# Windowed attention and a wave-MLP in one kernel: a new hand-written order with some copies on other engines

## The chip, the cores and the metric

The kernel runs on one core of a Trainium2 chip. The metric is the device time of one execution in microseconds; the median of three runs of the kernel before is 164.15 us (164.02 to 164.84).

## The reference

Four batches of 768 tokens and 8 heads of 64 go through attention and then through a mixing layer of width 512.

```python
scores = scale * np.matmul(q, k.transpose(0, 1, 3, 2))
is_global = pos[None, :] < 8
is_local = (rel >= 0) & (rel < 96)
dist = np.where(is_global & ~is_local, 96.0, np.abs(rel))
a = softmax(where(is_global | is_local, scores - slope[h] * dist, -1e9))
x = (a @ v), heads side by side                  # 768 x 512
theta = x @ w_theta
y = w_tok_r @ (x * cos(theta)) + w_tok_i @ (x * sin(theta))
u = x + y
out = u + np.maximum(u @ w_ch, 0.0)
```

A query sees itself, the 95 tokens before it and the first 8 tokens, so of the 768 x 768 scores only the diagonal tiles of 128 x 128 and the tiles beside them are computed.

## The kernel before

**Tiles.** Tokens are cut into 6 tiles of 128, heads into 4 pairs. Tokens are the partitions of x, u and the outputs; for the matmuls x and u are needed transposed (xT, uT). Batches are called 0 to 3.

**The order.** All five engines follow one order that is written out as a string at line 574. Each word names an operation and its indices: `s.1.2.0` calls `s_(1, 2, 0)`. The words are issued from left to right, and each engine runs its own instructions in that sequence. A second string at line 640 gives, word by word, the PSUM bank (of eight) that the next operation with a result in PSUM takes. An operation whose bank is still being read waits for that reader.

**Words, by stage.** b is the batch, p the head pair, i is 0 for q and 1 for k, and the letter v or a at the end names VectorE or ScalarE as the engine of a copy.

- Loads, issued by POOL (GpSimd): `lq` q and k (lines 77 and 86), `lv` v (line 92), `lw`, `lt`, `lc` the weights. Batch 3 is loaded token by token, in 16 transfers (`lq.3.0.4` and `lq.3.4.4`). Only q and k of batch 0, pair 0 come through SP and ScalarE's queue (line 103). `mv` (line 212) writes the column of ones of v before v is loaded.
- Bias: batch 0 adds the distance bias on TensorE (`sb`, lines 336 and 343, from `diag` and `dist`); the others multiply the exponentials by a table (`bt` makes it on ScalarE, line 153; `x` multiplies on VectorE, lines 383 and 386).
- `cast` (line 276) turns q and k of pair 0 to bf16. `q` (lines 291 and 294) transposes q or k on TensorE; `pc` (line 306) packs for that. `qe` (line 299) copies the result from PSUM to qT or kT; its last number is 2 for the whole and 0 or 1 for a half of the tokens. `pd` (line 312) does both for batch 3 as a transposing transfer issued by SP.
- `kg` (lines 322 and 323) makes kG: a copy of kT's tiles in which the first 8 columns are the global tokens, in two instructions for the tiles t0 to t1. `vg` (lines 397 and 398) does the same for v.
- `s` (line 362) computes scores into two banks, in three pieces c per head pair; `e` (line 374) is the exponential on ScalarE; `v` (line 421) multiplies by v, and `n` (lines 432 and 434) divides by the sum on VectorE and writes x.
- `xt` (line 451) transposes a pair of x on TensorE and `xe` (line 456) copies it; `xd` (line 443) does both as one transposing transfer issued by SP. x of batch 2, pair 3 goes by `xt.2.3` and `xe.2.3`; its pairs 0 to 2 go by `xd`.
- `w` and `we` (lines 265 and 269) transpose and copy the token weights, in batch 0.
- `th` (line 477) is theta, `sn` (lines 487 and 489) cosine and sine on ScalarE, `z` (line 498) the products on VectorE, `m` (line 511) the mixing over tokens, in three groups g for each output tile tt, `u` (line 519) the sum on VectorE. `sin` (line 257) is a sine of one column, which brings the activation table ahead.
- u is transposed by `ut` and `ue` (lines 535 and 539, TensorE and a copy) or by `ud` (line 529, a transposing transfer issued by SP). All of batch 0 goes by `ut`; so does the last tile, 3.5.
- `c` (line 550) multiplies by w_ch, `r` (line 560) does the maximum and the sum on VectorE, `st` (line 566) stores. The last number 2 is a whole tile of 128 x 512; 0 and 1 are its halves, and half 1 is stored from ScalarE's queue, the others from SP's. Only tile 3.5 goes in halves. `r` takes turns among 8 output buffers.
- `gt.1.2` (line 230) is a copy of one element of z of batch 1 on POOL. POOL stands there until z.1.1.0 has run, and `lq.3.4.4` is behind it.
- `warm` (line 237) are matmuls of zeros.

Of the kernel before, what the change touches and what calls it, by code (L numbers as in the profile page):

```python
# [16 lines left out]
def kernel(  # L17
# [105 lines left out]
    dist = const.tile([T, 6, T], BF)  # L123
# [13 lines left out]
    half = T // 2  # L137
# [6 lines left out]
    diag = const.tile([T, H, T], BF)  # L144
# [37 lines left out]
    ps_of = {}  # L182
# [147 lines left out]
    def sb_(p, c):  # L330
        pb = ps_of["s", 0, p, c] = ps_big()
        n = blocks(c)
        s0 = 2 if c else 0
        if p < 2:
            for hh in range(2):
                nc.tensor.matmul(pb[:, hh, 0:n * T], lhsT=diag[:, 2 * p + hh],  # L336
                                 rhs=dist[:, s0:s0 + n].rearrange("p s n -> p (s n)"),
                                 start=True, stop=False)
            return
# [8 lines left out]
    def s_(b, p, c):  # L348
        qT, kT, kG = qkT[b, p]
        if b:  # L350
            ps_of["s", b, p, c] = ps_big()
        pb = ps_of["s", b, p, c]
        for j in range(2):
# [3 lines left out]
            for part in range(2 if jt + 1 < NT else 1):  # L357
                for hh in range(2):
# [4 lines left out]
                                     start=bool(b), stop=bool(b) or (jt == NT - 1 or (j == 1 and part == 1)))  # L363
# [205 lines left out]
    def do(op, *a):  # L569
# [17 lines left out]
        xe.0.3.0.2.v bt.5 xt.0.2.0.6 xt.0.3.4.6 bt.3 xe.0.2.0.6.v th.0.0.4 we.0.0.v lv.1.0.8 bt.2
        we.1.0.v th.0.0.5 mv.2 th.0.0.3 we.1.1.v th.0.1.2 we.0.1.v sn.0.0.0 xe.0.3.4.6.v lq.2.0.8
        w.2.0 sn.0.0.1 z.0.0.0 th.0.1.3 th.0.2.2 sn.0.1.0 z.0.0.1 sn.0.1.1 w.3.0 z.0.1.0 th.0.2.3
        w.2.1 sn.0.2.0 z.0.1.1 m.0.0.0 m.0.1.0 sn.0.2.1 z.0.2.0 lv.2.0.8 w.3.1 pc.1.1.0 sin.0  # L590
        m.0.1.1 we.2.0.a z.0.2.1 we.3.0.a pc.1.0.0 m.0.0.1 q.1.1.0 we.2.1.v m.0.1.2 bt.1 q.1.0.0
        pc.1.0.1 m.0.2.0 qe.1.0.0.a.2 pc.1.1.1 qe.1.1.0.v.2 q.1.0.1 q.1.1.1 qe.1.0.1.a.2 m.0.0.2
        pc.1.3.0 pc.1.2.0 kg.1.0.0.4.a pc.1.3.1 q.1.3.0 u.0.1 m.0.2.1 qe.1.1.1.a.2 pc.1.2.1 we.3.1.v
        w.4.0 lq.3.0.4 kg.1.1.0.4.a u.0.0 q.1.2.0 m.0.2.2 qe.1.3.0.v.2 qe.1.2.0.a.2 ut.0.1 we.4.0.v
        s.1.0.0 ue.0.1.a s.1.0.1 u.0.2 w.4.1 e.1.0.0 w.5.1 we.4.1.v ut.0.0 q.1.2.1 e.1.0.1 ue.0.0.v
        q.1.3.1 qe.1.2.1.v.2 c.0.1.2 qe.1.3.1.a.2 we.5.1.v s.1.1.0 s.1.0.2 r.0.1.2 s.1.1.2 e.1.1.0
        c.0.0.2 kg.1.2.0.4.a x.1.1.0 m.0.3.0 x.1.0.1 e.1.1.2 m.0.4.0 r.0.0.2 e.1.0.2 m.0.3.1 x.1.0.2
        x.1.0.0 s.1.1.1 s.1.2.0 e.1.1.1 vg.1.0.8 m.0.3.2 kg.1.3.0.4.a w.5.0 m.0.4.1 x.1.1.1 e.1.2.0
# [24 lines left out]
        z.2.2.1 s.3.0.2 m.2.0.1 st.0.3.2 r.1.5.2 e.3.0.2 m.2.1.2 e.3.0.1 x.3.0.2 vg.3.0.8 s.3.1.0
# [60 lines left out]
```

## Time and profile before

| what | value |
|---|---|
| median of three runs | 164.15 us (164.02 to 164.84) |
| the profiled execution's own time | 164.6 us |
| its span, first to last instruction | 162.4 us |
| granted TensorE clock over the span | 1.00 |
| first theta matmul | 25.4 us |
| last matmul's end, last VectorE result, last store landed | 158.6, 159.1, 161.2 us |
| u transposing transfers, issue to landing | 17, median 2.5 us |
| x transposing transfers, issue to landing | 8, median 3.0 us |

The span is what the engines' rows cover; the execution's own time has 2.2 us around it. "Busy" is the union of an engine's rows. A row of the timeline gives start, duration, engine, line, operation and tiles, and in brackets the idle time before it with what ended that. The times in this text count from the start of the span.

### The profile page before, as it was taken

What the parts mean: (1) busy time and instruction counts of PE and PEld (TensorE: products, weight loads), DVE (VectorE), ACT (ScalarE), POOL (GpSimd) and SP (SyncE); (2) the same over time, 40 slices, a digit from 0 to 9 for tenths busy, and PEclk for the clock granted to TensorE, in tenths of its full rate; (3) what the DMA queues carried; (4) which work ended last, traced back from release to release, by engine and by line L of the source; (5) the groups of instructions that cost most, each with busy time, mean ns of one, the idle gap of its engine ahead of it and who ended that gap; (6) DMA issues with size and microseconds to landing.
All of it is one profiled execution on the core that took longest, in us unless ns stands there. A gap on an engine that the chain in (4) does not pass through costs nothing.

```text
span 162.4 us, 3831 instructions
## 1 busy us (share of the span) xinstructions
PE 156.0 (96%) x1575; PEld 87.1 (54%) x1575; DVE 123.7 (76%) x254; ACT 110.9 (68%) x148; POOL 38.3 (24%) x46
## 2 busy tenths in 40 slices
PE   7979999999999999999999999999999999999990
PEld 2446686556845586454655554445464544444450
DVE  7688998686989998997989682896987714736371
ACT  3978999999987897989987776898560339100010
POOL 8985248104408202029900000000000000000000
PEclk9999999999999999999999999999999999999999
DMA  4999999999999999929999996660679086003885
GB/s 140 211 165 177 206 209 205 203 210 200 157 176 204 168 131 151 197 56 84 133 130 136 197 164 151 129 178 4 145 228 128 12 238 160 4 0 76 248 286 198
DMA packets 71904, 25.14 MB, mean 155 GB/s; under 512 B 59984, under 2 KB 68944, under 8 KB 71888
## 3 DMA queue, kind: packets, MB, share of 16 engines
q0 software_dynamic: 45696, 12.45, 89.4%
q1 hardware_dynamic: 25776, 11.93, 33.5%
q10 hardware_dynamic: 416, 0.52, 0.9%
q8 instruction: 12, 0.20, 0.5%
q14 instruction: 4, 0.03, 0.1%
HBM read 25.69 MB, written 6.29 MB: 197 GB/s over the span
## 4 chain that ended last, share of the span: by engine, by line
PE 89%; DVE 7%; issue 1%; ACT 0%; DVEq 0%
PE bank L511 39%; PE bank L477 13%; PE bank L550 12%; PE bank L421 6%; PE bank L362 6%; PE bank L294 3%; PE bank L237 3%; PE bank L265 3%; PE bank L451 2%; PE bank L336 1%; DVE kG L322 1%; DVE qT L299 1%; DVE x_sb L434 1%; PE bank L535 1%; DVE kT L299 1%
## 5 line engine op out<-in xcount | busy, mean ns | idle before, releaser
L511 PE MATMUL bank<-zri,w_tokT 128*128 128x512 bf16 x288 | 68.8, 379 | 0.0
L374 ACT ACTIVATE e<-bank 128x1024 bf16<-128x1024 f32 (+1 forms) x48 | 43.2, 955 | 8.1 <-PE bank L362 7.7
L511 PEld LDWEIGHTS <-w_tokT 128*128 128x128 bf16 x288 | 26.4, 98 | 28.2
L498 DVE TENSOR_TENSOR zri<-x_sb,cs 128x1024 bf16<-128x1024 bf16 (+1 forms) x30 | 16.6, 581 | 10.6 <-ACT cs L489 5.5
L550 PE MATMUL bank<-w_ch_bf,uT 128*128 128x512 bf16 (+1 forms) x100 | 24.0, 371 | 0.0
L519 DVE TENSOR_TENSOR u<-x_sb,bank 128x512 bf16<-128x512 bf16 x24 | 16.3, 682 | 9.1 <-PE bank L511 9.1
L477 PE MATMUL bank<-w_theta_bf,xT 128*128 128x512 bf16 x96 | 22.8, 379 | 0.0
L560 DVE SCALAR_TENSOR_TENSOR o<-bank,u 128x512 f32<-128x512 f32 (+1 forms) x25 | 16.5, 665 | 2.5 <-PE bank L550 2.5
L434 DVE TENSOR_TENSOR x_sb<-bank,rec 128x768 bf16<-128x768 f32 (+2 forms) x21 | 16.1, 767 | 0.7
L383 DVE TENSOR_TENSOR e<-e,etab 128x1024 bf16<-128x1024 bf16 (+1 forms) x24 | 14.8, 635 | 1.5 <-ACT e L374 1.5
L539 ACT COPY uT<-bank 128x512 bf16<-128x512 bf16 x4 | 2.4, 592 | 18.2 <-PE bank L535 18.2
L550 PEld LDWEIGHTS <-uT 128*128 128x128 bf16 x100 | 9.4, 98 | 10.1 <-DMA uT<-u 0.5
L477 PEld LDWEIGHTS <-xT 128*128 128x128 bf16 x96 | 9.1, 98 | 9.7 <-DVE xT L456 0.2
L421 PEld LDWEIGHTS <-e 128*128 128x128 bf16 x352 | 12.6, 97 | 2.8 <-issue 0.2
L362 PE MATMUL bank<-qT,kT 64*128 64x128 bf16 x224 | 13.4, 218 | 0.0
L421 PE MATMUL bank<-vn,e 128*128 128x65 bf16 x224 | 12.7, 193 | 0.2
L489 ACT ACTIVATE cs<-bank,halfpi 128x1024 bf16<-128x1024 f32 x8 | 8.9, 1114 | 5.6 <-PE bank L477 5.6
L362 PEld LDWEIGHTS <-kT 64*128 64x128 bf16 x224 | 8.7, 94 | 7.0 <-issue 6.1
L92 POOL DMA_DIRECT2D vn<-in_v_dram x5 | 9.9, 1976 | 8.0 <-DVE qkn L306 7.1
L362 PE MATMUL bank<-qT,kG 64*128 64x128 bf16 x128 | 10.4, 216 | 0.9 <-DVE kG L323 0.9
L421 PE MATMUL bank<-vG,e 128*128 128x65 bf16 x128 | 10.3, 193 | 0.0
L86 POOL DMA_DIRECT2D qk<-in_q_dram x8 | 6.9, 857 | 10.7 <-issue 5.4
(77 smaller groups left out, 206.4 us busy)
## 6 DMA issues: line engine op xcount, KB each, us to landing
out_dram<-o SPq DMA_DIRECT2D x23, 256.0 KB, 2.4
vn<-in_v_dram POOLq DMA_DIRECT2D x3, 768.0 KB, 23.4
qk<-in_q_dram POOLq DMA_DIRECT2D x2, 768.0 KB, 20.6
qk<-in_k_dram POOLq DMA_DIRECT2D x2, 768.0 KB, 22.0
w_nat<-in_moe_w_tok_r_dram POOLq DMA_DIRECT2D x3, 384.0 KB, 12.7
w_nat<-in_moe_w_tok_i_dram POOLq DMA_DIRECT2D x3, 384.0 KB, 13.8
vn<-in_v_dram POOLq DMA_DIRECT2D x2, 384.0 KB, 10.1
qk<-in_q_dram POOLq DMA_DIRECT2D x8, 96.0 KB, 7.4
```

Source lines behind the costliest of these rows:

```text
L92: nc.gpsimd.dma_start(out=vn[:, h0:h0 + n, :, 0:D].rearrange("p h t d -> p (h t) d"), in_=v[b, h0:h0 + n].rearrange("h (t p) d -> p (h t) ...
L362: nc.tensor.matmul(pb[:, hh, o:o + T], lhsT=lhsT, rhs=qT[R, (own, nxt)[part]], start=bool(b), stop=bool(b) or (jt == NT - 1 or (j == 1 and ...
L374: nc.scalar.activation(e_c, ps_of["s", b, p, c][:, :, 0:blocks(c) * T], AF.Exp, scale=scale)
L383: nc.vector.tensor_mul(e_c, e_c, tab[:, :, s0:s0 + n].rearrange("p a s n -> p a (s n)"))
L421: nc.tensor.matmul(po4[:, head - h0, it - i0], lhsT=l_, rhs=r_, start=(i_ == 0), stop=(i_ == len(mms) - 1))
L434: nc.vector.tensor_mul(xv, po4[:, :, :, 0:D], rec.to_broadcast([T, m_, nt, D]))
L477: nc.tensor.matmul(ps_of["th", b, c][j_], lhsT=xT_sb[b][:, dc, (2 * c + j_) * T:(2 * c + j_ + 1) * T], rhs=w_theta_bf[:, dc, :], start=(dc ...
L498: nc.vector.tensor_mul(zri[b][:, i_, tt, :].rearrange("p j (g d) -> p j g d", g=NP), x_sb[b][:, :, tt, :].rearrange("p g j d -> p j g d"), ...
L511: nc.tensor.matmul(ps_of["m", b, tt], lhsT=w_tokT[wi][:, st, tt * T:(tt + 1) * T], rhs=zri[b][:, wi, st, :], start=(mixed[b, tt] == 0), st ...
L519: nc.vector.tensor_add(u_sb[b, tt].rearrange("p (g d) -> p g d", g=NP), x_sb[b][:, :, tt, :], ps_of["m", b, tt].rearrange("p (g d) -> p g ...
L550: nc.tensor.matmul(ps, lhsT=uTs[b, tt][:, dc, :], rhs=w_ch_bf[:, dc, own], start=(dc == 0), stop=(dc == NC - 1))
L560: nc.vector.scalar_tensor_tensor(o_sbs[b, tt][:, own], in0=ps_of["c", b, tt, part], scalar=0.0, in1=u_sb[b, tt][:, own], op0=ALU.max, op1= ...
```

## The change

- Pair 0 of batch 0: the two halves of q are copied by VectorE (`qe.0.0.0.v`), those of k by ScalarE, and the first tile of kG is made by ScalarE (`kg.0.0.0.1.a`).
- The copy `gt.1.2` is gone; `lq.3.4.4` stands before `th.1.0.6`, and `mv.3` and `lv.3.0.8` come after `s.2.0.2`.
- u tile 0.1 goes by `ud.0.1`, x pair 2.3 by `xd.2.3`.
- The output tiles 3.1 and 3.2 are computed, finished and stored in halves, in the last stretch of the order.
- kG of batch 2, pair 0 is made in two parts. Some other copies change between VectorE and ScalarE.
- The order and the banks are written anew throughout. The sequence of operations of one engine differs in most places.
- `sb_` has a new branch that no word of the order uses, and `s_` asks whether its banks were taken already, which gives the same as before.

The diff, cut to the functions, the order up to the first theta matmul, and the places that the text speaks of:

```diff
@@ -327,10 +327,18 @@
         return min(4, 2 * NT - 1 - 4 * c)
 
     @op
-    def sb_(p, c):
+    def sb_(p, c, rows=False):
         pb = ps_of["s", 0, p, c] = ps_big()
         n = blocks(c)
         s0 = 2 if c else 0
+        if rows:
+
+            for hh, r in ((0, 0), (1, 1), (0, 1), (1, 0)):
+                K = slice(r * half, (r + 1) * half)
+                nc.tensor.matmul(pb[:, hh, 0:n * T], lhsT=diag[K, 2 * p + hh],
+                                 rhs=dist[K, s0:s0 + n].rearrange("p s n -> p (s n)"),
+                                 start=(r == hh), stop=False)
+            return
         if p < 2:
             for hh in range(2):
                 nc.tensor.matmul(pb[:, hh, 0:n * T], lhsT=diag[:, 2 * p + hh],
@@ -347,7 +355,8 @@
     @op
     def s_(b, p, c):
         qT, kT, kG = qkT[b, p]
-        if b:
+        fresh = ("s", b, p, c) not in ps_of
+        if fresh:
             ps_of["s", b, p, c] = ps_big()
         pb = ps_of["s", b, p, c]
         for j in range(2):
@@ -360,7 +369,7 @@
                     lhsT = kG[R, jt - 1, :] if part and jt else kT[R, own]
                     o = (2 * j + part) * T
                     nc.tensor.matmul(pb[:, hh, o:o + T], lhsT=lhsT, rhs=qT[R, (own, nxt)[part]],
-                                     start=bool(b), stop=bool(b) or (jt == NT - 1 or (j == 1 and part == 1)))
+                                     start=fresh, stop=fresh or (jt == NT - 1 or (j == 1 and part == 1)))
...
-        warm.3.1 diag.0 diag.1 dist warm.6.0 bt.6 swap bt.0 cast.1.0.v cast.1.1.a sb.0.0 bt.7 sb.0.1
-        cast.0.1.a cast.0.0.v q.0.0.1 q.0.1.0 qe.0.0.1.a.0 q.0.0.0 qe.0.1.0.a.2 kg.0.0.0.1.v
-        warm.1.3 qe.0.0.1.v.1 qe.0.0.0.a.0 kg.0.0.1.4.v q.0.1.1 qe.0.0.0.a.1 s.0.0.0 lw.0
-        qe.0.1.1.v.2 s.0.0.1 e.0.0.0 sb.1.2 sb.1.0 kg.0.1.0.4.v lt.0.2 e.0.0.1 diag.2 s.0.1.0
-        q.0.2.1 lt.2.4 e.0.1.0 q.0.2.0 qe.0.2.1.v.2 s.0.1.2 sb.0.2 e.0.1.2 sb.1.1 kg.0.2.0.4.v
-        s.0.1.1 qe.0.2.0.v.2 sb.2.1 e.0.1.1 lw.2 s.0.0.2 vg.0.0.4 sb.2.0 e.0.0.2 q.0.3.0 diag.3
-        s.0.2.0 mv.1 s.0.2.1 qe.0.3.0.v.2 e.0.2.0 q.0.3.1 lq.1.0.8 sb.2.2 qe.0.3.1.v.2 e.0.2.1
-        v.0.1.1.0.6 v.0.1.0.0.6 v.0.0.0.0.6 n.0.1.1.0.6 kg.0.3.0.4.a v.0.0.1.0.6 s.0.2.2 n.0.0.1.0.6
-        sb.3.0 e.0.2.2 s.0.3.0 vg.0.4.4 sb.3.1 e.0.3.0 sb.3.2 n.0.0.0.0.6 s.0.3.1 s.0.3.2 e.0.3.1
-        v.0.2.0.0.6 n.0.1.0.0.6 v.0.3.2.0.2 v.0.2.1.0.6 lw.4 n.0.3.2.0.2 e.0.3.2 xt.0.1.0.6
-        v.0.3.2.2.4 n.0.2.0.0.6 xt.0.0.0.6 xe.0.1.0.6.a v.0.3.2.4.6 n.0.3.2.2.4 warm.1.2 w.0.0 bt.4
-        n.0.2.1.0.6 xt.0.3.2.4 w.0.1 xe.0.0.0.6.a w.1.0 n.0.3.2.4.6 xt.0.3.0.2 xe.0.3.2.4.a w.1.1 lc
...
-        w.4.0 lq.3.0.4 kg.1.1.0.4.a u.0.0 q.1.2.0 m.0.2.2 qe.1.3.0.v.2 qe.1.2.0.a.2 ut.0.1 we.4.0.v
-        s.1.0.0 ue.0.1.a s.1.0.1 u.0.2 w.4.1 e.1.0.0 w.5.1 we.4.1.v ut.0.0 q.1.2.1 e.1.0.1 ue.0.0.v
...
-        xt.1.3.0.6 r.0.2.2 kg.2.0.0.4.a th.1.0.6 xe.1.3.0.6.v th.1.2.0 r.0.3.2 pd.3.0.0 th.1.0.3
...
-        sn.1.1.1 z.1.1.0 th.1.2.3 pc.2.3.0 m.1.0.0 sn.1.2.0 pc.2.3.1 gt.1.2 z.1.1.1 q.2.2.1 lq.3.4.4
...
-        s.2.1.1 ud.1.0 e.2.1.0 s.2.1.2 q.2.2.0 kg.2.2.0.4.v lv.3.0.8 m.1.2.0 x.2.0.1 e.2.1.1 ud.1.1
...
-        xt.2.3.0.6 th.2.0.6 xe.2.3.0.6.a th.2.1.6 st.0.2.2 th.2.0.3 ud.1.5 th.2.2.0 sn.2.0.0
...
-        ud.3.1 u.3.2 r.2.3.2 m.3.4.1 ud.3.0 c.2.4.2 u.3.4 c.3.1.2 ud.3.2 r.2.4.2 m.3.3.2 st.2.2.2
-        m.3.5.0 st.2.3.2 st.2.5.2 m.3.3.1 ud.3.4 m.3.5.2 u.3.3 r.3.1.2 c.3.2.2 ud.3.3 m.3.5.1
...
-        c.3.4.2 ue.3.5.a st.3.3.2 c.3.5.1 r.3.4.2 c.3.5.0 r.3.5.1 st.3.4.2 r.3.5.0 st.3.5.1 st.3.5.0
-        760254766461026407627106462540176432513704562450176325470103124063276240632560460240620532
...
+        warm.3.1 diag.1 dist warm.6.0 diag.0 bt.0 swap bt.6 cast.1.1.a cast.0.0.v sb.0.1 cast.0.1.a
+        sb.0.0 bt.5 cast.1.0.v q.0.0.0 bt.7 qe.0.0.0.v.1 q.0.0.1 qe.0.0.0.v.0 sb.1.0 qe.0.0.1.a.0
+        qe.0.0.1.a.1 q.0.1.1 kg.0.0.0.1.a kg.0.0.1.4.v q.0.1.0 lw.0 qe.0.1.1.a.2 s.0.0.0 s.0.0.1
+        e.0.0.0 warm.1.3 kg.0.1.0.4.v lt.0.2 qe.0.1.0.v.2 q.0.2.1 e.0.0.1 sb.0.2 lt.2.4 diag.2
+        s.0.1.0 qe.0.2.1.v.2 s.0.0.2 e.0.1.0 sb.1.1 kg.0.2.0.4.v q.0.2.0 e.0.0.2 s.0.1.1
+        qe.0.2.0.v.2 sb.1.2 e.0.1.1 lw.2 sb.2.0 diag.3 s.0.2.0 vg.0.0.4 sb.2.1 e.0.2.0 s.0.1.2
+        s.0.2.1 v.0.0.0.0.6 e.0.1.2 lq.1.0.8 q.0.3.1 n.0.0.0.0.6 q.0.3.0 e.0.2.1 sb.2.2 qe.0.3.1.v.2
+        v.0.0.1.0.6 qe.0.3.0.a.2 v.0.1.0.0.6 n.0.0.1.0.6 s.0.2.2 sb.3.0 e.0.2.2 kg.0.3.0.4.v
+        v.0.1.1.0.6 n.0.1.0.0.6 bt.3 s.0.3.0 sb.3.1 vg.0.4.4 e.0.3.0 s.0.3.1 sb.3.2 n.0.1.1.0.6
+        s.0.3.2 e.0.3.1 v.0.2.0.0.6 v.0.2.1.0.6 lw.4 n.0.2.0.0.6 w.0.0 e.0.3.2 v.0.3.2.0.2
+        xt.0.0.0.6 n.0.2.1.0.6 we.0.0.a v.0.3.2.2.4 v.0.3.2.4.6 n.0.3.2.0.2 xe.0.0.0.6.a w.0.1
+        n.0.3.2.2.4 xt.0.2.0.6 bt.2 xt.0.1.0.6 n.0.3.2.4.6 xt.0.3.0.2 warm.1.2 xe.0.2.0.6.a w.1.1
+        xe.0.1.0.6.v lc xt.0.3.4.6 w.1.0 we.0.1.v bt.1 xt.0.3.2.4 xe.0.3.0.2.v xe.0.3.4.6.a th.0.0.4
...
+        lq.2.0.8 we.2.1.a m.0.1.0 we.3.1.v sn.0.1.1 z.0.1.0 m.0.2.0 pc.1.1.0 sin.0 sn.0.2.0 lv.2.0.8
...
+        pc.1.1.1 pc.1.0.1 q.1.0.0 u.0.1 bt.4 q.1.1.1 q.1.0.1 qe.1.0.0.v.2 ud.0.1 m.0.0.1
...
+        q.1.2.0 e.1.0.1 ue.0.0.v m.0.3.0 qe.1.2.0.v.2 s.1.1.0 x.1.0.1 s.1.1.2 e.1.1.0 c.0.1.2
...
+        qe.2.1.1.a.2 th.1.1.0 n.1.3.2.0.6 kg.2.1.0.4.a ut.0.5 th.1.0.0 r.0.2.2 xt.1.3.0.6 lq.3.4.4
+        th.1.0.6 kg.2.0.0.1.v xe.1.3.0.6.v th.1.2.0 pc.2.2.0 pc.2.3.0 vg.2.0.8 th.1.0.3 th.1.1.6
...
+        sn.1.1.0 z.1.0.1 th.1.2.3 m.1.0.0 sin.1 sn.1.1.1 z.1.1.0 kg.2.0.1.4.v m.1.1.0 sn.1.2.0
...
+        z.1.2.1 s.2.0.0 s.2.0.2 mv.3 m.1.1.2 e.2.0.0 lv.3.0.8 m.1.0.2 u.1.1 e.2.0.1 q.2.3.0 u.1.0
...
+        xd.2.3 th.2.1.0 vg.3.0.8 th.2.0.6 pd.3.1.1 th.2.1.6 sin.2 x.3.0.0 th.2.2.0 ud.1.3 c.1.5.2
...
+        st.2.2.2 c.3.4.2 r.3.3.2 st.2.4.2 ut.3.5 st.3.3.2 r.3.4.2 c.3.1.1 ue.3.5.a c.3.2.1 r.3.1.1
+        st.3.4.2 c.3.5.0 r.3.2.1 st.3.1.1 c.3.1.0 r.3.5.0 st.3.2.1 c.3.5.1 r.3.1.0 st.3.5.0 c.3.2.0
+        r.3.5.1 st.3.1.0 r.3.2.0 st.3.5.1 st.3.2.0
+        760254654552046241036214026105432105476326140276235435102764070426732407350643040240635403
...
```

## The prediction

> **What bounds the kernel now.** I read the engine totals first, then the chain of work that ended last, then TensorE's waits, then the stages of the span.
>
> ```profile
> PE 156.0 (96%) x1575; PEld 87.1 (54%) x1575; DVE 123.7 (76%) x254; ACT 110.9 (68%) x148; POOL 38.3 (24%) x46
> DMA  4999999999999999929999996660679086003885
> PE 89%; DVE 7%; issue 1%; ACT 0%; DVEq 0%
> ```
>
> ```profile
> 0.00:25.00 25.00, 22.38 (x360) 14.10 (x361) 20.94 (x61) 20.23 (x29) 16.23 (x24) 1.00 1.35 185
> 25.00:47.00 22.00, 22.00 (x213) 13.51 (x211) 17.55 (x41) 21.27 (x31) 7.82 (x6) 1.00 1.76 190
> 118.00:140.00 22.00, 22.00 (x168) 11.10 (x163) 13.97 (x24) 9.92 (x12) 0.00 (x0) 1.00 0.64 141
> ```
>
> The second fence is busy time by stretch (PE, weight loads, DVE, ACT, POOL). From 25 us on TensorE is busy in all of every stretch, at a granted clock of 1.00. So three things can move the end: TensorE's own work, what it loses before 25 us, and the tail. The rest of the new order counts only where it makes TensorE wait. In the prologue one wait stands out:
>
> ```profile
> PE bank L362 <- DVE kG L323: 0.9, 1, 0.9
> ```
>
> ```profile
> 7.34 1.46 POOL L92 DMA_DIRECT2D vn<-in_v_dram  x1
> 7.63 1.19 DVE L322 COPY kG<-kT 128x128 bf16<-128x128 bf16 x1 [1.26 <-ACT kT L299]
> 8.94 0.55 DVE L299 COPY kT<-bank 128x384 bf16<-128x384 bf16 x1
> 9.81 0.40 DVE L323 COPY kG<-kT 128x24 bf16<-128x24 bf16 x1
> 10.27 0.23 PE L362 MATMUL bank<-qT,kG 64*128 64x128 bf16 x2 [0.90 <-DVE kG L323]
> ```
>
> The first kG copy needs 1.19 us, though the 128x512 copy of the same line takes 0.28 at 79.04. It starts under POOL's v load and ends 0.02 us after that load's issue (7.34 + 1.46 = 8.80). The kT copy behind it (0.55) and the rest of kG (to 10.21) follow, and TensorE's scores start at 10.27.
>
> **Prologue.** kG's first block goes to ScalarE. No row shows 128x128 there; its 128x512 takes 0.62 and its 128x32 0.22 (both at 18 us). So the two copies cost between 0.4 and 0.85; I take 0.5, near the small one. If ScalarE waited out the load as VectorE did, they would end at about 9.0 instead of 8.9. I walk the new order with durations from the rows. ScalarE: k halves to 8.4, kG to 8.9, kT of pair 1 (0.80) to 9.65, so the first exponential starts at 9.6 (before: 9.36). VectorE: q halves (0.55 each) to 8.2, kG's other blocks held to 8.8 by the same load and done at 9.2. TensorE: pair 1's k lands at 8.15, its transposes take it to 8.9, and the first two score pieces of pair 0 are done at 9.5. Before, they were done at 10.6; 0.43 of bias matmuls (sb.1.0) was then still to come, and in the new order 0.22 (warm.1.3) is.
>
> This lead of 1.3 us shrinks, because the next limits are others. q of pair 1 is copied by 11.0, so e.0.1.0 starts at 11.45 (before 11.98). ScalarE then has exponentials of 0.90 and 0.71 each from start to start, plus one q copy and one table that stood elsewhere, and ends e.0.3.2 at 21.75 (before 22.42). VectorE's last division ends at 23.6 (24.92). Behind e.0.3.2 ScalarE still has we.0.0, xe.0.0, bt.2 and xe.0.2 (3.0 together), and the first theta matmul takes the bank that xe.0.2 frees: 24.7, against 25.42. **Prologue: -0.7.** Bounds: -1.1 if only TensorE's rows and VectorE's counted (24.3), -0.2 if one 0.5 copy more falls on the chain. Five more changes of tile shape come in before that point (29 for 24); the next fence prices one at 0.1, and they lie in the waits that remain.
>
> **TensorE work.** Pieces of the chain (start, us, what):
>
> ```profile
> 42.22 0.22 PE bank L535 x4
> 46.27 0.97 PE bank L550 x4
> 97.43 0.34 PE bank L451 x6
> 101.22 1.73 PE bank L550 x8
> ```
>
> ut.0.1 goes (-0.22) and xt.2.3 goes (-0.34). An output tile in halves is eight matmuls, 2 x 0.43 at 157.5 to 158.4, against 1.73 / 2 = 0.865; two such tiles cost +0.02. The tile behind scores takes 0.97 instead of 0.865, which is the 0.1 for a change of shape; from the first theta matmul on I count 28 changes in both orders. **Work: -0.54**, all on the path, since TensorE has no slack there.
>
> **Edits that I cost at nothing, with their cover.** The x pair 2.3 by transfer: v's end, 0.2, division 1.19, issue and landing 2.75 (its neighbour at 91.9): 4.2, at most 4.6 with ud.1.5's issue ahead on SP; TensorE has 5.6 us of other work between, so 1.0 is spare, and every us beyond costs a us. pd.3.1.1, ud.1.3 and the first batch's stores now queue behind it on SP; r.1.2 needs the buffer of st.0.1.2, which lands about 1 us before it. Copies changing between VectorE and ScalarE leave the summed durations of their rows (overlaps counted twice) at 135.7 (136.0) and 107.1 (107.4). The tightest stage, batch 1's scores up to xt.1.1, has, by count times row, 16.8 us of TensorE against 16.5 of VectorE and 14.4 of ScalarE (before 17.1, 16.9, 15.9, and no wait); splitting kG of pair 2.0 adds 0.4 to VectorE later, where it has 1 us spare. Halved outputs: r takes 0.41 for every 0.43 of matmul, and a half store lands in 2.1 as now, so the tail keeps its length.
>
> The gate copy (0.25) held POOL 8.1 us. Without it q/k of heads 4 to 7 of batch 3 are issued at about 64.5 instead of 72.3 (8 x 0.85) and v's load at 74.8 instead of 78.8, behind the moved mv.3. The transposes that read these q/k are issued from about 79 on, v is read near 99, and TensorE waited for none of them: 0. v's issue (2.35) held three VectorE results to 81.14 without stopping TensorE; in its new place u and a copy from PSUM run, and such rows (0.68, 0.95) kept their time under it. mv.1, lv.1 and lq.2 are issued some 3.5 us later; the queue is full until 42, so nothing lands later.
>
> **The u tile 0.1 by transfer** is the unknown. u.0.1 ends at about 38.1, SP is free, and TensorE wants uT at 45.2. Transposes of u took 2.4 us with idle queues, 4.8 beside loads at 78.5. The only one in the loads' dense stretch is x pair 1.0:
>
> ```profile
> L443 SPq DMA_TRANSPOSE xT<-x_sb x1: 1309/1309/1309, 54.6 to 54.6; - x1
> DMA to landing us min/median/max: 7.9/7.9/7.9
> ```
>
> It is half again as long as a u tile. Bounds for ud.0.1 are 2.4 and 7.9: landing at 40.5 to 46.0, so no wait or 0.8. I take 5.5 (two thirds of 7.9, rounded up): no wait. Its engines are taken from v's load of batch 1 (landed 48.45), needed at 49.1: some 1.5 us later would leave VectorE idle and v.1.0 0.3 late. The Trainium skill (DMA: Bandwidth & Descriptors, Queues, rings and completion order) says that each engine takes turns between its queues. By turns I would estimate twice 2.4, landing at 42.9, and a sum as mine; the 7.9 of x pair 1.0, against 2.7 alone, is worse than turns, and by it alone the sum would be 0.8 higher.
>
> For this and the other places with under 0.1 to spare (m.0.2.0 behind we.2.1, q.1.3.0 behind pc.1.3.0) I set **+0.2**.
>
> **Sum.** -0.70 - 0.54 + 0.20 = -1.04. The profiled execution took 164.6 us, 2.2 around its span of 162.4; the change gives 163.6 there. The median shown is 164.15, 0.45 less, so I forecast **163.1**, its own range 162.5 to 163.6.
>
> **Rivals.**
> - The prologue's gain is eaten: ScalarE, which now has kG, kT and a q copy before its exponentials, runs 0.5 later than walked. For it: its chain sets 24.7. Against it: 0.7 earlier at e.0.3.2. Total -0.5: 163.6.
> - The u transfer takes x pair 1.0's 7.9: c.0.1.2 waits 0.8, total -0.25: 163.9.
> - **Slower:** the u transfer gets through only when the load beside it is through. For it: x pair 1.0 landed at 62.44, the v load then running at 62.85; xd.2.0 at 91.67, its v load at 91.04. Against it: ud.1.0 beside lighter loads took 4.8. Here v of batch 1 lands at 48.45; c.0.1.2 would start at 48.5 instead of 45.2, +3.3, total +2.2: 166.3. It decides from a landing at about 47.1, where the gain and the 0.5% are both gone.
> - All small waits stay out and the prologue reaches its -1.1: -1.6, 162.5.
>
> **Chances.** Forecast 0.58, gain eaten 0.10, 7.9 us transfer 0.08, slower 0.14, all out 0.10. 0.5% of 164.15 is 0.82 us, about what a measurement can tell, so faster means under 163.33. Three quarters of the forecast's case lie there: 0.44 + 0.10 = 0.54. Same: 0.14 + 0.10 + 0.08 = 0.32. Slower 0.14. The range for 8 in 10 is 162.3 to 165.0; it leaves out most of the slow case and the best end.
>
> **What would show it.** The first kG copy on ScalarE ends before 9.1, and no wait of 0.9 for kG stands in TensorE's list. The first theta matmul starts at 24.3 to 25.0. TensorE's pieces from there to its end are 0.5 shorter. uT of tile 0.1 lands before 45 and L550's weight load does not wait for it. From the last matmul's end to the end of the span it stays 3.8. I am wrong if waits for VectorE, ScalarE or a transfer above 0.3 appear between 25 and 155, or if the theta matmuls do not start earlier.

## The result and the profile after

The changed kernel takes **166.97 us** (median of 4 runs) against 164.50 us for the kernel before on the same chip: ratio 1.015, 95% interval 1.011 to 1.019. It is 2.5 us slower; the forecast was 163.1 us. In the execution profiled first (170.53 us) TensorE's granted clock was only 0.55 and 0.60 in the stretches 102 to 104 and 104 to 106 us, right behind the wait at theta that is described below, so the rows shown are those of a repeat of the same kernel (span 164.6 us).

First the totals, the DMA line of the 40 slices, and the chain of work that ended last, of the changed kernel:

```profile
PE 155.1 (94%) x1573; PEld 86.6 (53%) x1573; DVE 123.5 (75%) x257; ACT 109.9 (67%) x147; POOL 38.8 (24%) x45
DMA  4999999999999999999999997983503674005776
PE 73%; DMA 16%; DVE 5%; POOL 2%; ACT 1%; issue 1%; POOLq 0%; DVEq 0%
```

TensorE's share of the chain has gone from 89% to 73%, and transfers, which had none worth printing, have 16%. The stretches say where (columns as before: PE, weight loads, DVE, ACT, POOL):

```profile
0.00:25.00 25.00, 22.63 (x370) 14.25 (x371) 21.26 (x64) 22.07 (x32) 16.26 (x24) 1.00 1.36 187
25.00:47.00 22.00, 21.03 (x193) 12.48 (x191) 17.34 (x41) 19.53 (x28) 7.96 (x6) 1.00 1.83 183
80.00:102.00 22.00, 19.13 (x215) 10.57 (x214) 16.87 (x34) 14.22 (x18) 0.00 (x0) 1.00 1.48 135
118.00:140.00 22.00, 22.00 (x192) 11.34 (x187) 14.92 (x25) 11.56 (x15) 0.00 (x0) 1.00 0.46 109
```

From 25 to 47 TensorE is idle for 1.0, from 80 to 102 for 2.9; before it was busy in all of both. Its list of waits names them:

```profile
PE bank L486 <- DMA xT<-x_sb: 1.7, 1, 1.7
PE bank L371 <- DVE e L395: 1.1, 1, 1.1
PE bank L559 <- DMA uT<-u: 1.0, 1, 1.0
```

The first matmul after each stands 1.89, 1.29 and 1.14 later than usual, counted from start to start: theta of batch 2 at 97.59, the first scores of batch 3 (`s.3.0.0`) at 91.89, the output of u tile 0.1 at 44.65.

**The account.** From the first theta matmul to the end of the last matmul the kernel before has 158.57 - 25.42 = 133.15 us, the changed one 161.34 - 24.43 = 136.91: +3.76. The three waits make 4.32, so by this account TensorE's work has become 0.56 shorter. Theta began 0.99 earlier in this pair of executions, and the tail from the last matmul to the end is 3.23 instead of 3.81. Together +2.19, the difference of the spans.

### The profile page after: what moved, and what is told of

The parts are those of the page before. It is cut to its first block, busy times and chain, and to the rows that moved or that the text cites. A ratio compares the mean times of both kernels' runs of the same rounds, so it can differ in the third digit from the quotient of the medians.

```text
span 168.6 us, 3812 instructions
## 1 busy us (share of the span) xinstructions
PE 156.6 (93%) x1551; PEld 87.3 (52%) x1573; DVE 126.3 (75%) x257; ACT 110.0 (65%) x147; POOL 38.5 (23%) x45
## 4 chain that ended last, share of the span: by engine, by line
PE 63%; DMA 18%; ACT 7%; DVE 6%; POOL 3%; issue 2%; POOLq 0%
PE bank L520 28%; PE bank L486 12%; PE bank L559 11%; DMA qk<-in_k_dram 6%; DMA uT<-u 5%; DMA kT<-qk 4%; PE bank L371 4%; PE bank L430 4%; DMA xT<-x_sb 3%; POOL qk L77 2%; PE bank L294 2%; ACT cs L498 2%; DVE o L569 2%; ACT cs L496 1%; ACT e L383 1%
## 5 line engine op out<-in xcount | busy, mean ns | idle before, releaser
L520 PE MATMUL bank<-zri,w_tokT 128*128 128x512 bf16 x273 | 66.2, 379 | 1.0 <-issue 0.3
L486 PE MATMUL bank<-w_theta_bf,xT 128*128 128x512 bf16 x93 | 24.2, 401 | 2.2 <-DMA xT<-x_sb 2.0
L392 DVE TENSOR_TENSOR e<-e,etab 128x1024 bf16<-128x1024 bf16 (+1 forms) x24 | 14.3, 617 | 3.0 <-ACT e L383 3.0
L559 PEld LDWEIGHTS <-uT 128*128 128x128 bf16 x108 | 10.2, 98 | 10.2 <-DMA uT<-u 1.0
L548 ACT COPY uT<-bank 128x512 bf16<-128x512 bf16 x5 | 3.0, 605 | 18.5 <-PE bank L544 18.5
L430 PE MATMUL bank<-vn,e 128*128 128x65 bf16 x224 | 13.5, 193 | 0.3 <-DVE x_sb L443 0.3
```

The lines of the kernel that those rows point to most:

```text
L392: nc.vector.tensor_mul(e_c, e_c, tab[:, :, s0:s0 + n].rearrange("p a s n -> p a (s n)"))
L430: nc.tensor.matmul(po4[:, head - h0, it - i0], lhsT=l_, rhs=r_, start=(i_ == 0), stop=(i_ == len(mms) - 1))
L486: nc.tensor.matmul(ps_of["th", b, c][j_], lhsT=xT_sb[b][:, dc, (2 * c + j_) * T:(2 * c + j_ + 1) * T], rhs=w_theta_bf[:, dc, :], start=(dc ...
L520: nc.tensor.matmul(ps_of["m", b, tt], lhsT=w_tokT[wi][:, st, tt * T:(tt + 1) * T], rhs=zri[b][:, wi, st, :], start=(mixed[b, tt] == 0), st ...
L559: nc.tensor.matmul(ps, lhsT=uTs[b, tt][:, dc, :], rhs=w_ch_bf[:, dc, own], start=(dc == 0), stop=(dc == NC - 1))
```

## Where the two large waits come from

The name "DVE e" on the second wait is the releaser that ended last by the profile, but TensorE's first row after it starts at 93.19, and the transposed q that it needs too landed at 93.05. In experiment 3 the multiplication of that name ends at 93.79, 0.74 after those scores have started, so it is not what they wait for. SP's own queue shows why so late (start, duration):

```profile
77.96 1.20 SPq L538 DMA_TRANSPOSE uT<-u  x1
79.33 1.31 SPq L312 DMA_TRANSPOSE kT<-qk  x1
80.75 5.42 SPq L312 DMA_TRANSPOSE qT<-qk  x2
86.36 1.58 SPq L312 DMA_TRANSPOSE kT<-qk  x1
87.99 1.59 SPq L538 DMA_TRANSPOSE uT<-u  x1
89.68 2.92 SPq L452 DMA_TRANSPOSE xT<-x_sb  x1
92.70 1.21 SPq L538 DMA_TRANSPOSE uT<-u  x1
94.01 2.57 SPq L452 DMA_TRANSPOSE xT<-x_sb  x2
```

Rows of 1.2 are the usual length. `pd.3.0.0` alone is issued from 82.42 to 86.18. Everything behind it on SP is late: `xd.2.2`, whose x was finished at 91.13, is issued at 95.34 and lands at 99.42; theta starts at 99.47. The DMA part of the window from 76 to 100 us gives the transfers' median times from issue to landing:

```profile
vn<-in_v_dram POOLq DMA_DIRECT2D x1, 768.0 KB, 15.7
kT<-qk SPq DMA_TRANSPOSE x2, 7.9
qT<-qk SPq DMA_TRANSPOSE x2, 9.8
```

Batch 3's v load (`lv.3.0.8`) is issued at 76.07 and lands at 91.74. In the old order `pd.3.0.0` and `pd.3.1.1` ran at 65 to 71, in the quiet stretch that the gate copy kept, and `pd.3.2.0` and `pd.3.2.1` after 100. The new order issues `pd.3.2.0`, `pd.3.0.0` and `pd.3.2.1` at 80 to 88, with `pd.3.3.1`, u and x transfers around them (`pd.3.1.1` follows at 100), and most of these stand in this load. The kernel before has transfers beside this load as well, and they are shorter. From its window of 76 to 100 us:

```profile
vn<-in_v_dram POOLq DMA_DIRECT2D x1, 768.0 KB, 12.2
kT<-qk SPq DMA_TRANSPOSE x1, 5.5
```

The four that it has there took 4.8 (`ud.1.0`), 4.8 (`ud.1.1`), 6.2 (`xd.2.0`) and 5.5 (`pd.3.3.1`), and TensorE waited for none of them.

**Theory 1:** beside a v load a transposing transfer takes 7 to 11 us instead of 2.4 to 2.8 and holds SP's queue, and the words moved into that stretch are what costs 2.5 us net. **Rivals:** ScalarE's idle 5.7 us before kG of batch 3's pair 2 is the loss and the transfers only happen to end last; SP's order costs the same with or without the load; the lost gate is the loss.

## The experiments

Times are given with the ratio to the kernel before on the same chip. In the diffs a line is a piece of the order.

**1. The changed kernel again**, for its profile. No edit.

> The changed kernel once more, for an undisturbed profile. Theory 1 (the crowd: five of the transposing transfers of batch 3's q and k and of u now stand on SP while v of batch 3 is loading, take 8 to 11 us each instead of 2.8, and hold up SP's queue, so that x pairs 2.x and q of pair 3.0 come late): 166.6 to 167.0, the two waits of about 1.4 us at scores of batch 3 and 2.2 us at theta of batch 2 show again. Theory 2 (the waits belong to the run that was profiled, and the loss is spread over the order): 166.6 to 167.0 too, but no wait for a transfer above 0.7 us.

The four runs took 165.98, 166.52, 168.49 and 168.69 us, beside a median of 163.90: even the shortest is 2.1 over it, so the loss is there. The profile above is that of the run of 166.52.

**2. Four batch-3 transfers moved,** three of them out of the load (`pd.3.1.1` was already behind it). The changed kernel with

```diff
- q.2.2.0 q.2.3.1 pd.3.2.0 e.2.1.2
+ q.2.2.0 q.2.3.1 e.2.1.2
- m.1.3.0 x.2.0.0 pd.3.0.0 qe.2.3.1.a.2
+ m.1.3.0 x.2.0.0 qe.2.3.1.a.2
- s.2.2.2 m.1.2.2 pd.3.2.1 x.2.1.2
+ s.2.2.2 m.1.2.2 x.2.1.2
- xd.2.1 c.1.0.2 kg.3.2.0.4.a m.1.5.1
+ xd.2.1 c.1.0.2 m.1.5.1
- vg.3.0.8 th.2.0.6 pd.3.1.1 th.2.1.6
+ vg.3.0.8 th.2.0.6 th.2.1.6
+ vg.2.0.8 pd.3.0.0 th.1.0.3
+ th.1.2.6 pd.3.1.1 pc.2.2.1
+ pd.3.1.0 pd.3.2.1 pd.3.2.0 sn.2.1.0
+ m.2.1.2 e.3.0.2 kg.3.2.0.4.a
```

> The changed kernel with four of the transfers of batch 3's q and k taken out of v's load: pd.3.0.0 and pd.3.1.1 go ahead of it, as in the kernel before, pd.3.2.1 and pd.3.2.0 behind pd.3.1.0, and kg.3.2 with them. Theory 1: the waits at batch 3's first scores and batch 2's theta shrink below 0.5 us in all, 162.8 to 164.0. Theory 2 (spread over the order): within 0.5 us of the changed kernel, 166.3 to 167.3.

163.71 us, ratio 1.000 (0.997 to 1.003). From 26 us on TensorE's list holds only these:

```profile
PE bank L559 <- DMA uT<-u: 0.8, 1, 0.8
PE bank L294 <- DVE qkn L306: 0.6, 1, 0.6
```

Both large waits are gone, and with them the whole loss against the kernel before. The u wait of tile 0.1 stays. `ud.1.0`, `pd.3.3.1` and `ud.1.1` still stand in the load and took 7.8, 8.3 and 9.5 us, but nothing on TensorE waits for them, and `xd.2.2` lands at 96.19. So a long transfer costs nothing by itself; the loss came from q of pair 0, which the scores need, and from the x pairs queued behind it.

**3. Only kG moved**, so that ScalarE doesn't wait; every transfer stays.

```diff
- xd.2.1 c.1.0.2 kg.3.2.0.4.a m.1.5.1
+ xd.2.1 c.1.0.2 m.1.5.1
+ m.2.1.2 e.3.0.2 kg.3.2.0.4.a
```

> The changed kernel with one word moved: the kG copies of batch 3's pair 2 stand behind the exponentials of s.3.0.2 on ScalarE, so ScalarE no longer sits idle for 5.74 us until that pair's k transfer has landed; all transfers stay where they are. Theory 1 (the loss is the transfers themselves: pd.3.0.0 and xd.2.2 land late, one beside the v load, the other behind SP's row of issues): TensorE's waits of 1.29 at s.3.0.0 and 1.89 at theta of batch 2 stay to within 0.5, and the time stays at 166 to 167.5. Rival (the loss is ScalarE's idle time, and the transfers that the profile names only ended last by little): both waits go and the time falls by 2 to 3, to 164 or 164.5.

166.88 us, ratio 1.015 (1.012 to 1.019): no gain. Between 90 and 101 us TensorE's list now names the transfers themselves:

```profile
PE bank L486 <- DMA xT<-x_sb: 1.9, 2, 1.5
PE bank L371 <- DMA qT<-qk: 0.4, 1, 0.4
```

The wait at `s.3.0.0` fell from 1.29 to 0.55, by more than I had allowed, but not because of ScalarE: u tile 0.1's wait, far from the edit, rose from 1.14 to 1.72, so TensorE came to these scores 0.6 later, and q landed at 92.91 instead of 93.05. In both runs the scores start 0.14 after q has landed. Theta's wait rose from 1.89 to 2.23, in two pieces. ScalarE's idle time was not what set the end.

**4. The load moved, the transfers not.** `gt` reads x of batch 2's pair 2 here instead of z, so GpSimd issues the v load only at 92.56.

```diff
-        nc.gpsimd.tensor_copy(out=gate, in_=zri[b][0:1, 0, j, 0:1])
+        nc.gpsimd.tensor_copy(out=gate, in_=x_sb[b][0:1, j, 0, 0:1])
...
- m.1.1.2 e.2.0.0 lv.3.0.8 m.1.0.2
+ m.1.1.2 e.2.0.0 m.1.0.2
+ m.1.4.0 n.2.2.2.0.6 gt.2.2 lv.3.0.8
```

> The changed kernel with batch 3's v load held back on GpSimd by a one-element copy that reads x of batch 2's pair 2, so that it is issued at about 91 to 93 us instead of 76.07; SP's order stays. Theory 1 (beside the load each transposing transfer takes 7 to 11 us instead of 2.4 to 2.8, and SP's issues stretch): pd.3.3.1, pd.3.2.0, pd.3.0.0 and pd.3.2.1 land within 3.5 us of their issue, SP is free before 90, TensorE's wait of 1.29 at s.3.0.0 and ScalarE's idle 5.74 at kG of pair 2 go, and xd.2.2 is issued within 1 us of its x; the x pairs then stand in the load themselves, so the 1.89 wait may stay or grow to 4. Time between 164.3 (both waits gone) and 167.5 (the x pairs' wait grows). Rival (SP's queue order alone, whatever the load does): the landings stay at 7 to 11 us from issue and the 1.29 wait stays within 0.3.

169.45 us, ratio 1.029 (1.024 to 1.034), above the 167.5 that I had as the upper end. The same transfers in the same order, from 76 to 92 us:

```profile
uT<-u SPq DMA_TRANSPOSE x3, 2.7
kT<-qk SPq DMA_TRANSPOSE x2, 3.6
qT<-qk SPq DMA_TRANSPOSE x2, 2.8
xT<-x_sb SPq DMA_TRANSPOSE x2, 3.2
```

q takes 2.8 instead of 9.8 (of the four batch-3 transfers only `pd.3.2.1` needed more, 4.4); `pd.3.0.0` is issued in 1.23 instead of 3.76; `xd.2.2` goes out 0.2 after its x; of TensorE's waits, those at `s.3.0.0` and theta are gone, and so is ScalarE's at kG. So SP's order by itself does not make these two waits: without the load the same row of transfers took 2.4 to 4.6. What then stood in the load was `ud.1.5`, issued at 95.75 and landed at 104.98 (9.2 us), and TensorE waited 5.16 for it: the loss moved with the load. The list shows it, as the longest of two waits:

```profile
PE bank L559 <- DMA uT<-u: 5.8, 2, 5.0
```

Not all of the 169.45 is that wait. Behind it the granted clock was 0.68 from 104 to 106 us and 0.50 from 106 to 108, and the 512-wide matmuls there started 0.43 us apart instead of 0.22. From these rows I estimate 1.5 us for it. It seems to come up in every run: the four have a mean granted clock of 0.98 to 0.99, the 23 runs of the kernel before beside them 0.995 to 1.00. I had not reckoned with that, and it is part of why the time lies above my range.

**5. The crowd alone, in the old order,** with the gate out first:

```diff
- sn.1.2.0 pc.2.3.1 gt.1.2 z.1.1.1 q.2.2.1 lq.3.4.4 m.1.0.1
+ r.0.2.2 kg.2.0.0.4.a lq.3.4.4 th.1.0.6
```

> The kernel before without the gate copy, q and k of heads 4 to 7 of batch 3 issued ahead of th.1.0.6, nothing else changed. Theory 1: the three transfers that the kernel before issues at 65 to 69.5 us now run beside those loads and take 5 us instead of 3, but v's load and what stands under it stay as they were: within 0.5 us of the kernel before. Theory 3 (the gate alone is the loss): 166 to 167.

and then the transfers moved as in the change:

```diff
- th.1.2.0 r.0.3.2 pd.3.0.0 th.1.0.3
- th.1.2.6 pc.2.2.1 pd.3.1.1 sn.1.1.0
- z.2.1.0 th.2.2.3 pd.3.2.1 c.1.2.2
- sn.2.2.1 z.2.2.0 pd.3.2.0 c.1.5.2 kg.3.2.0.4.v r.1.2.2
...
+ lv.3.0.8 m.1.2.0 pd.3.3.1 x.2.0.1
+ x.2.1.0 q.2.3.1 pd.3.2.0 e.2.1.2
+ s.2.2.1 m.1.3.0 pd.3.0.0 e.2.2.0
+ x.2.1.2 v.2.0.2.0.6 ud.1.1 e.2.2.1 m.1.2.2 pd.3.2.1
+ x.2.2.0 c.1.0.2 kg.3.2.0.4.v e.2.3.0
+ xt.2.3.0.6 th.2.0.6 pd.3.1.1 xe.2.3.0.6.a
```

> The kernel before, without the gate copy, and with the transfers of batch 3's q and k on SP, ud.1.1 and the copy kg.3.2 in the changed kernel's places; all else is the kernel before. Theory 1: it loses as the changed kernel does, 165.5 to 168, with waits for a transfer at batch 3's scores or batch 2's theta. Theory 2 (spread over the order): within 0.7 us of the kernel before.

Without the gate: 165.40 us, ratio 1.008 (1.004 to 1.012), 1.5 above the kernel before, where I had allowed 0.5. With the crowd too: 167.61, ratio 1.021 (1.017 to 1.026). TensorE's list of the second:

```profile
PE bank L511 <- DVE o L560: 1.9, 1, 1.9
PE bank L511 <- DVE zri L498: 1.3, 1, 1.3
```

The 1.3 is in both, and is the missing gate: the v load's issue moved from 78.8 to 71.2-73.6 us. Of two packing copies on VectorE the second, started at 71.62 under that issue, took 2.08 instead of 0.35, and z behind it started only at 73.62, when the issue had ended (73.55). The 1.9 is the crowd, by a neighbouring road: kG of pair 2 is on VectorE in the old order, and VectorE waited 2.19 until `pd.3.2.1` landed at 89.86, with `r.1.0.2` behind it. There the load was already in (81.41) and transfers took 2.8 to 4.1: this loss is the queue's order, not the load. So the old order pays for the move too, but does not repeat the mechanism of the new one, and this pair is only half a confirmation.

**6. u tile 0.1 turned on TensorE again,** on top of experiment 2.

```diff
- qe.1.0.0.v.2 ud.0.1 m.0.0.1
+ qe.1.0.0.v.2 m.0.0.1
+ q.1.2.1 m.0.0.2 ut.0.1 we.4.0.a
+ m.0.2.2 u.0.0 ue.0.1.v qe.1.2.1.a.2
```

> The spread order, with u tile 1 of batch 0 turned on TensorE again (transposes behind m.0.0.2, their copy on VectorE behind u.0.0) instead of by a transfer. Theory: the wait of 0.65 to 1.14 us at 44.65 in the first output product is that transfer, which took about 8 us to land in batch 2's and v's loads; with the transposes the wait goes and 0.22 us of TensorE work comes back: 162.8 to 163.2, 0.5 to 0.9 below the spread order on the same footing. Rival: the product then waits for something else, the GELU of tile 1 or the copy of the transposes, and the time stays at 163.7 or rises by the 0.22.

163.51 us, ratio 0.996 (0.993 to 1.000), a little above my 162.8 to 163.2. The same kernel once more:

> The spread order with TensorE's transposes of u tile 0.1 once more, beside the three others: 0.3 to 0.6 below before.

163.07 us, ratio 0.995 (0.992 to 0.998), beside 164.17 for the kernel before: 1.1 below, more than I expected. The wait of 0.8 to 1.0 at the first output is gone and nothing took its place. (The kernel has no GELU; that word in the rival names nothing in it.) In six executions of the orders that have it, this transfer took 8.0 to 8.9 us from issue to landing. In the changed kernel, its issue in SP's timeline, and then the time to landing from the view of its line:

```profile
37.38 1.30 SPq L538 DMA_TRANSPOSE uT<-u  x1
```

```profile
DMA to landing us min/median/max: 8.4/8.4/8.4
```

**7. The gate copy put back,** on top of experiment 6.

```diff
- r.0.2.2 xt.1.3.0.6 lq.3.4.4 th.1.0.6
+ r.0.2.2 xt.1.3.0.6 th.1.0.6
+ sn.1.1.1 z.1.1.0 gt.1.2 lq.3.4.4 kg.2.0.1.4.v
```

> The spread order with TensorE's transposes of u tile 0.1, and the gate copy put back: GpSimd waits for z.1.1.0 before it issues the q and k loads of batch 3's last pairs. Theory 1 (the quiet window that the gate keeps is worth something only where transposing transfers stand in it, and in this order three do: pd.3.0.0, pd.3.0.1 and pd.3.1.1): their landings fall from 6.4 to 6.9 us to 2.8 to 4, but nothing on TensorE waits for them, so the time is unchanged within 0.3 of the run without the gate. Rival (the gate was the loss): 0.5 or more faster than without. Or the loads that the gate holds back push the v load behind them later, into the x pairs: slower by 1 or more.

163.02 us, ratio 0.994 (0.991 to 0.997), beside 163.07 without. The three early transfers took 2.7 to 3.6 us instead of 6.9 to 7.4, and TensorE, which waited for none of them, gained nothing that can be measured. Both versions are 0.5 to 0.6% faster than the kernel before. That comes near the forecast's gain, but not by its terms: in the profile of this experiment the span is 1.15 shorter than before, of which theta's earlier start makes 0.47 (the start moves by over 1 us from execution to execution), the tail 0.52, which was forecast at 0, and the stretch between them 0.17.

**8. The first pair's engines put back,** on top of experiment 2.

```diff
- qe.0.0.0.v.1 q.0.0.1 qe.0.0.0.v.0 sb.1.0 qe.0.0.1.a.0 qe.0.0.1.a.1 q.0.1.1 kg.0.0.0.1.a
+ qe.0.0.0.a.1 q.0.0.1 qe.0.0.0.a.0 sb.1.0 qe.0.0.1.a.0 qe.0.0.1.v.1 q.0.1.1 kg.0.0.0.1.v
```

> The spread order with the first pair's copies on the engines that they had before: q halves on ScalarE, the second k half and the first kG block on VectorE. Prediction's theory: the kG copy is then held by GpSimd's v load (1.19 us), TensorE waits 0.9 for it, and the end is 0.5 to 0.7 later: 164.2 to 164.4. Rival, from the traces since: in the two other executions with the old engines the first kG copy took 0.20 us at 7.25 and theta began at 24.61 and 24.39, in three with the new ones at 25.45, 24.43 and 25.39, so the 0.9 wait belonged to one execution and the engines are worth nothing: within 0.4 of the spread order's 163.71.

165.05 us, ratio 1.005 (1.002 to 1.007), against 1.000 (0.997 to 1.003) with the new engines: 0.5%, though the two intervals just touch. The first exponential starts at 10.02 instead of 9.30 (9.29 to 9.90 in eight executions with the new engines). So by the times the engines are probably worth something within the new order, against the rival (nothing). But the mechanism of the theory is not there: the first kG copy starts at 8.99, behind the load's issue (7.20 to 8.63), and takes 0.36; TensorE's list has no wait for kG, and theta starts at 25.29, earlier than in three executions with the new engines (25.39 to 25.45). Where the 0.5% comes from stays open. In the old order the old engines start the first exponential at 8.79 to 9.36, so against that the new prologue gains nothing; the starts of theta below say the same.

**9. The tail alone, and the x pair alone,** in the old order. First tiles 3.2 and 3.4 in halves at the end:

```diff
- r.3.1.2 c.3.2.2 ud.3.3 m.3.5.1 r.3.2.2 c.3.0.2 st.3.2.2 u.3.5 st.3.1.2 c.3.3.2 r.3.0.2 st.2.4.2 ut.3.5
- st.3.0.2 r.3.3.2 c.3.4.2 ue.3.5.a st.3.3.2 c.3.5.1 r.3.4.2 c.3.5.0 r.3.5.1 st.3.4.2 r.3.5.0 st.3.5.1 st.3.5.0
+ r.3.1.2 ud.3.3 m.3.5.1 c.3.0.2 u.3.5 st.2.4.2 st.3.1.2 r.3.0.2 c.3.2.1 st.3.0.2 ut.3.5 c.3.4.1 r.3.2.1
+ ue.3.5.a c.3.3.2 r.3.4.1 st.3.2.1 c.3.5.0 r.3.3.2 st.3.4.1 c.3.4.0 r.3.5.0 st.3.3.2 c.3.5.1 r.3.4.0
+ st.3.5.0 c.3.2.0 r.3.5.1 st.3.4.0 r.3.2.0 st.3.5.1 st.3.2.0
```

> The kernel before with only its tail changed: the output products of tiles 3.2 and 3.4 in halves at the end, between those of tile 3.5, everything up to there as before. The prediction's theory: the tail from the last matmul to the end stays at 3.8 and two more outputs in halves cost 0.02, so nothing changes: within 0.2. Rival, from the traces since: with the last outputs all halves VectorE is no longer behind when TensorE ends, and the tail was 3.20 to 3.28 in every execution of the new order against 3.79 to 3.81 in three of the old: 0.5 to 0.6 faster.

164.16 us, ratio 0.999 (0.997 to 1.001). The tail fell from 3.81 to 3.59, not to 3.2, and the time does not show it. Then, on top, x pair 3 of batch 2 by a transfer:

```diff
- ud.1.3 xt.2.3.0.6 th.2.0.6 xe.2.3.0.6.a th.2.1.6 st.0.2.2 th.2.0.3 ud.1.5 th.2.2.0
+ ud.1.3 th.2.0.6 th.2.1.6 st.0.2.2 th.2.2.0 th.2.2.6 th.2.0.3 ud.1.5
+ m.1.4.2 n.2.3.2.0.6 xd.2.3 sin.3
```

> As before_halves, and x pair 3 of batch 2 turned by a transfer instead of six TensorE transposes, with the two pieces of theta that don't need it put ahead of the one that does. The transfer has about 3 us and needs 2.8 where SP is free. If it is free: a further 0.3 faster than before_halves (six transposes of 0.50 together out, less a gap), 0.8 to 0.9 below before. If SP's other issues or the u transfer behind it make theta or the outputs of batch 1 wait: no faster than before_halves, or slower by up to 1.

164.93 us, ratio 1.005 (1.003 to 1.007): 0.8 slower than the halves alone. `xd.2.3` itself took 2.7 us and theta did not wait for it, but it waits on SP for its x until 96.69 and holds `ud.1.3` behind it, which was issued at 97.95, in the kernel before at 95.18. Waits of 0.67 (for a u transfer) and 0.36 (for an exponential) came up, more than the 0.34 that six transposes cost.

## Why the prediction was wrong, by its steps

**The step that failed** is the one under "Edits that I cost at nothing": "The transposes that read these q/k are issued from about 79 on, v is read near 99, and TensorE waited for none of them: 0." The issue times came out right (79 to 88). The term of 0 did not: in the trace of before most of these transfers stood elsewhere, so that nobody waited for them said nothing about their new place. I moved the v load and the transfers onto each other in the same sentence without giving the transfers a new duration, though the row of 7.9 for x pair 1.0 beside a load lay in front of me for the u tile, and though the same profile has the four rows of 4.8 to 6.2 beside this very load (I called the loads beside `ud.1.0` lighter, but the v load is issued 0.26 after it). Measured in place of the 0: the three moved transfers took 7.4 to 10.6 us, SP's queue was late by up to 4.2, and TensorE waited +1.29 at `s.3.0.0` and +1.89 at theta, far above the +0.2 that I had set aside for small waits. Experiment 2 takes both away; 3 and 4 show that the transfers, lengthened by the load, made them. What sets a transfer's length there, how many stand in the queue or how far into the load it is issued, was not tried separately.

**The x pair 2.3** was held to have 1.0 to spare. Right for that pair: it landed at 101.62 without a wait. But `xd.2.2` ahead of it on the same queue was late, and I had walked only the pair that the change adds.

**The u tile 0.1.** I took 5.5 us from issue to landing; it took 8.4. The wait was 1.14 instead of none. The mechanism is that of my second rival, and its row, 7.9, was the right size; I had set a value between two bounds without a row for it. The slower rival, a landing when v is through, did not happen: u landed at 45.74, v of batch 1 at 50.56. That v was held to land as before, because the queue is full until 42; it landed 2.1 later than its 48.45, and VectorE stood 1.5 us for it, but TensorE's list has no wait there.

**TensorE's work** of -0.54 came out as -0.56 by the account above, which puts every small loss into this term.

**The prologue** of -0.70 came out as -0.99 in the executions compared, but that was luck. Its first steps went as walked: the two kG copies on ScalarE took 0.31 and 0.20 and were done at 8.59, and the first exponential started at 9.34 (walked: 9.6). But theta started at 25.42, 24.61, 24.39, 24.64 and 25.54 in five executions with the old prologue, and at 25.45, 24.43, 25.39, 24.46, 24.55, 25.41, 24.95 and 24.74 in eight with the new: the mean is 24.92 for each. The 0.9 wait for kG that I built on is there in two of the five. In another (the second of experiment 5) the same copy took:

```profile
7.24 0.20 DVE L322 COPY kG<-kT 128x128 bf16<-128x128 bf16 x1 [0.87 <-ACT kT L299]
7.34 1.45 POOL L92 DMA_DIRECT2D vn<-in_v_dram  x1
```

It starts 0.10 before the load's issue and takes 0.20; in the profile that I read it started 0.29 after and took 1.19. The new prologue can't meet that collision with its first block, but in the late ones of its executions TensorE waits 0.5 to 0.7 for a q/k load. If its engines are worth something within the new order (experiment 8), the rest of the new prologue gives that back; this was not tried by itself.

**The gate at 0** was right for the repaired new order (experiment 7) and would have been wrong by 1.3 us for the old one (5), where copies ahead of z run while the load is issued.

**The tail at 0** was wrong by 0.58 on the good side: in eight further executions of orders built on the new one it lasts 3.21 to 3.29, in three of the old one 3.79 to 3.81. From the last matmul's end the last store lands after 2.31 instead of 2.67 (VectorE is 0.04 behind TensorE instead of 0.11), and the span ends 0.92 after that instead of 1.14. Two outputs in halves give 0.2 in the old order (experiment 9); what gives the rest is not settled.

## What to carry to other kernels

A transfer that nobody waits for has a price only in the place where it stands: before moving one, look for a row of its kind beside the load that it will meet, and take at least that row's duration for every transfer queued there and for the queue behind them. A wait read off one execution has a chance as well as a size: find out whether it starts from a collision of a tenth of a microsecond before counting on its removal. And when one transfer is added to a queue, walk those ahead of it and behind it, not only its own cover.

## What the runs showed of the hardware

- Transposing transfers from SP beside one v load (768 KB): 4.8 to 6.2 us from issue to landing in the kernel before, 5.2 to 10.6 in the changed one, alone 2.4 to 2.8; SP's issue row was up to 3.8 instead of 1.2 long. The Trainium skill (DMA: Bandwidth & Descriptors, Queues, rings and completion order) says that an engine takes turns between its queues, a packet at a time; by that an estimate would be twice the time alone, 4.8 to 5.6. The four of the kernel before took about twice as long as alone, which agrees; those of the changed kernel took up to 3.8 times as long, which does not.
- A VectorE copy within the on-chip memory that starts while GpSimd issues a v load can be held until that issue ends. Of the copies in the fourteen profiles those that started up to 0.23 us into the issue's row ran at full speed (kG 128x512 at 79.04 in the kernel before, 0.28), those from 0.26 on were held to its end unless under 0.25 us of it was left (kG 128x128 at 7.60 in the second of experiment 9, 1.20). Copies from PSUM were not held (0.55 at 7.55 in experiment 5). Besides kG it hits the copies of `pc.1` at 36 us: in the first fence below the second of the three is held. Their rows in the second run of experiment 6, and then in experiment 7:

```profile
35.55 2.63 DVE L306 COPY qkn<-qk 128x768 bf16<-128x768 bf16 x3
35.55 2.21 POOL L92 DMA_DIRECT2D vn<-in_v_dram  x1 [2.12 <-DMA qk<-in_k_dram]
```

```profile
35.76 0.89 DVE L306 COPY qkn<-qk 128x768 bf16<-128x768 bf16 x3
36.28 2.21 POOL L92 DMA_DIRECT2D vn<-in_v_dram  x1 [2.63 <-DMA qk<-in_k_dram]
```

  In the first TensorE then waits 0.7, in the second not at all. The Trainium skill (SBUF — State Buffer, Who interferes with whom) says that when a VectorE instruction in a mode with two ports, which a copy can enter, meets a GpSimd instruction, the one that is issued first keeps the shared port pair for its whole length and the other is blocked. The held copies agree; whether GpSimd ever waited for a copy these rows don't settle.
- After a long wait TensorE's granted clock can fall. It was 0.50 for 3.4 us behind the wait of 5.16 in experiment 4 and behind one of 2.2 at theta in the first profile of the changed kernel, where thirteen matmuls of theta took 4.67 us instead of 2.98. Behind the wait of 1.89 in the repeat it stayed at 1.00. Where the limit lies was not tried.
- Executions of one kernel lie 1.5 to 2.3 us apart here: 30 spans of the kernel before between 161.3 and 162.8 us, 12 of experiment 6's between 160.7 and 163.0. The two collisions above, 0.9 and 0.7 us on TensorE, are of that size; that they make the whole of the spread was not shown.
